# Another place for one weight tile, another order for sums and loads, in a three-stage fused kernel

## The chip, the cores and the metric

The kernel runs on one core of a Trainium2 chip. The metric is the device time of one execution in microseconds; the median of three runs before the change is 1219.49 us (1219.48 to 1224.46).

## What is computed

Three layers in float32, one after another, all in one program:

```python
# attention, q, k, v of 4 batches x 8 heads x 576 x 64, blocks of 64
attn = softmax(where(block_i >= block_j, q @ k.T / 8, -1e9));  y = attn @ v
x = y.transpose(0, 2, 1, 3).reshape(2304, 512)
# first block: 512 -> 768 -> 512
h = maximum(maximum(x @ w1, x @ w2), x @ w3);  x = h @ w_out
# second block: four experts, 512 -> 1024 -> 512
for e in range(4):  out += p[:, e:e+1] * (maximum(x @ w1[e], 0) @ w2[e])
```

## The kernel before

A float32 product is made of three matmuls: each operand is split into a rounded high part and the low rest, and high by high, high by low and low by high are added up in PSUM. Weights are kept split that way.

**Attention and the first block.** Attention goes by pairs of heads: 4 batches of 4 pairs (n = 0 to 15, NALL = 16). For a pair come scores (L159), minima on VectorE (L224), exponentials on ScalarE (L231), scaling by the row sums on GpSimd (L257), transposes on TensorE (L285) and the product with v (L320). While the pairs of batch b + 1 run, the first block of batch b (`moe1`, L547) fills TensorE's gaps: a generator cut into units of about four matmuls, and `filler.upto` (L698) says after each step of a pair how many units shall have been traced. `LAG` (L16) and a term that grows with n hold it back. The scheduler places instructions by priority (order of tracing) and by its own simulated times; each engine and each queue then works strictly in the placed order. `tc.issue_after(x)` queues what its block traces behind x, for instructions on the engine of x alone.

A batch in `moe1` has 18 tiles of its hidden layer: for weights w1, w2, w3 (n = 0, 1, 2) and rows ff = 0 to 5, each 12 matmuls (`mm3`, L488) of 128x512 into one of two PSUM banks. The eviction is a copy on ScalarE for n = 0 (L562) and a running maximum on VectorE for n = 1, 2 (L564). Then `moe1_out` (L537) makes the output in four parts d = 0 to 3, 18 matmuls each. Weight tiles come by DMA from the split copies `held` (L474), all on the SP queue: `wt` and `wu` (five buffers together) for the hidden layer, `wo` (two buffers) for the output layer.

**The fourth batch's first block** (`moe1_last`, L584) uses seven products of half-size blocks in place of eight (Strassen's scheme in Winograd's form), for 384 of its columns at a time; the columns that do not fit take a second, narrower run (`rh`, `wu`) of 18 matmuls per d. It needs sums and differences of weight blocks. These are made earlier by `sums(g, w0, w1)` (L516), for g = 0 to 8 (g = 3 * (ff // 2) + n), from the two weight tiles of rows ff - 1 and ff: two adds of 128x512 on VectorE (L522), four of 128x256 (L524 to L527), a rounding copy on ScalarE (L530), a subtraction on VectorE (L531), and a 1 MB store to `summed` (L532). They are worked out in places of the arena that are free then, the future results of batches 1 and 2. Batch 1 makes g = 0, 2, 4, 6, 8, batch 2 makes g = 1, 3, 5, 7. The adds are traced when the second tile of the pair has been evicted, but nothing binds them to that; the rounding copy is queued behind the next tile's eviction. In `moe1_last` the sums of a group come back into the places of `xh`, `xl` (8 KB per partition each) and two more in turn (L611 to L622); the ninth group uses `xh`. The output layer of the fourth batch takes its four tiles from the two `wo` buffers in turn, so d = 2 follows d = 0 and d = 3 follows d = 1.

**The second block** begins with e = 0. `hidden2` (L1013) makes seven products of six matmuls for a pair of row blocks n, `second` (L1074) the other layer. `weights_in(e, n)` (L970) loads e_w1[e, n] (512 KB) into one scratch tile `t`, makes three combinations on VectorE (L949 to L952), rounds on ScalarE (L956), subtracts on VectorE (L958) into one of two tiles `w`, and stores the result to `ka` (L982) for later passes. `weights_out(e, n)` (L985) does the like for e_w2[e, n] (load L988 into a part of `part`, results in `w2` and `part`), with GpSimd for the subtraction. `part` (L1343) is one tile of 3072 columns; it begins where `xh` began, and `xl` follows `xh`. Its pool `pe` has `reuse_waits="tile"`: a tile of it waits for the earlier tiles that it overlaps. Before, `weights_in(0, 1)` is traced at L1321, its load behind the last load of the first block.

Of the kernel before, what the change touches and what calls it, by code (L numbers as in the profile page):

```python
# [7 lines left out]
F32R = mybir.dt.float32r  # L8
# [4 lines left out]
ALU = mybir.AluOpType  # L13
AX = mybir.AxisListType

LAG = 9  # L16
# [5 lines left out]
P = 128  # L22
# [5 lines left out]
def program(tc, q, k, v, w123, w_out, probs, e_w1, e_w2, out):  # L28
    nc = tc.nc

    B, H, D, S = k.shape[0], 2 * k.shape[1], k.shape[2] // 2, k.shape[3]
# [3 lines left out]
    KD = DM // P  # L35
    NF = FF // P
    NPAIR = H // 2
# [5 lines left out]
    def f(ap):  # L43
        return ap.bitcast(F32)
# [16 lines left out]
    arena = big.tile([P, KD * NT], F32, name="arena")  # L61
    x2f = [arena[:, b * KD * S:(b + 1) * KD * S].rearrange("p (d s) -> p d s", d=KD) for b in range(B)]
    dram = root.enter_context(tc.tile_pool(name="dram", bufs=1, space=bass.MemoryType.DRAM))
    held = [dram.tile([P, 2, NF * P], F32, name=f"held{i}") for i in range(3 * NF + KD)]
    summed = [dram.tile([P, 2, 4, 2 * P], F32, name=f"summed{i}") for i in range(3 * NF // 2)]
# [11 lines left out]
    mp = moe.enter_context(tc.tile_pool(name="moe", bufs=1))  # L77
    MAIN = 512
# [7 lines left out]
    NGRP = 3 * NF // 2  # L86
# [10 lines left out]
    pairs, later, made, exps, normal, least = {}, [], {}, [], [], []  # L97
# [259 lines left out]
    for n, src in enumerate(tiles):  # L357
        A = src.shape[1]
# [102 lines left out]
    def moe_weight(b, n, at=0, a0=0):  # L461

        if b == 0:
            return convert.weight(n)
        A = tiles[n].shape[1]
        wide = n >= 3 * NF
        if b == B - 1 and not wide:
            if at == 0:
                taken[0] = 0
            if at % WT >= 3:  # L470
                wide = True
                taken[0] += 1
        wt = weight_tile(n, wide)
        made["load"] = nc.sync.dma_start(  # L474
            out=f(wt[:, :, a0:A].rearrange("p k a f -> p k (a f)")), in_=held[n][:, :, a0 * P:A * P]
        )
        return wt
# [15 lines left out]
    UNITS = 3 * NF * 3 + KD * 5  # L493
# [21 lines left out]

    def sums(g, w0, w1):  # L516

        o = (2 - (g // 2 % 2) * (g % 2 == 0)) * KD * S
        high, raw = (arena[:, o + i * 8 * P:o + (i + 1) * 8 * P] for i in range(2))
        for i, w in enumerate((w0, w1)):  # L520
            x = [w[:, j].rearrange("p a f -> p (a f)") for j in range(2)]
            nc.vector.tensor_tensor(raw[:, i * 4 * P:(i + 1) * 4 * P], f(x[0]), f(x[1]), op=ALU.add)  # L522
        a11, a12, a21, a22 = (raw[:, i * 2 * P:(i + 1) * 2 * P] for i in range(4))
        nc.vector.tensor_tensor(a22, a21, a22, op=ALU.add)  # L524
        nc.vector.tensor_tensor(a21, a11, a21, op=ALU.subtract)
        nc.vector.tensor_tensor(a11, a22, a11, op=ALU.subtract)
        nc.vector.tensor_tensor(a12, a12, a11, op=ALU.subtract)  # L527
        behind = yield
        with tc.issue_after(behind.ins):
            nc.scalar.copy(high.bitcast(F32R), raw)  # L530
        nc.vector.tensor_tensor(raw.bitcast(F32R), raw, high, op=ALU.subtract)  # L531
        nc.sync.dma_start(  # L532
            out=summed[g].rearrange("p x s f -> p (x s f)"), in_=arena[:, o:o + 16 * P]
        )
        yield

    def moe1_out(b, runs):  # L537
# [9 lines left out]
    def moe1(b):  # L547
        hidden = [mp.tile([P, NF, MAIN], F32R, name=x, tag=x) for x in ("hh", "hl")]
        hh, hl = ([x[:, ff] for ff in range(NF)] for x in hidden)
        xh, xl = xs[b]  # L550
        prev, last, under = {}, {}, []
        if b:
            order = [(2 * j + i, n) for j in range(NF // 2) for n in range(3) for i in range(2)]
        else:
            order = [(ff, n) for ff in range(NF) for n in range(3)]
        for at, (ff, n) in enumerate(order):
            wt = moe_weight(b, 3 * ff + n, at)
            m = ps_m.tile([P, 512], F32, name="m", tag="m")[:, 0:MAIN]
            yield from mm3(m, [(wt[:, 0, d], wt[:, 1, d], xh[:, d], xl[:, d]) for d in range(KD)])
            if n == 0:  # L560
                prev[ff] = mp.tile([P, MAIN], F32, name="mt", tag="mt", bufs=3)
                ins = nc.scalar.copy(prev[ff], m)  # L562
            else:
                ins = nc.vector.tensor_tensor(prev[ff], m, prev[ff], op=ALU.max)  # L564
            if under:
                under.pop().send(ins)
            t = prev[ff]
            if n == 2:
                nc.gpsimd.tensor_scalar(hh[ff], t, 1.0, 0.0, op0=ALU.mult, op1=ALU.add)
                nc.gpsimd.tensor_tensor(hl[ff], t, f(hh[ff]), op=ALU.subtract)  # L570
            if b and ff % 2:
                g = 3 * (ff // 2) + n
                if g % 2 == b - 1:
                    under.append(sums(g, last[0], wt))
                    next(under[0])
            last[0] = wt
            yield
        yield from moe1_out(b, [(MAIN, hh, hl, lambda d: x2f[b][:, d, 0:MAIN])])
        for x in under:
            x.send(made["out"])  # L580

    begun = [0]

# [126 lines left out]
    NALL = B * NPAIR  # L710
    filler = Filler()
# [24 lines left out]
    for n in range(NALL):  # L736
        b, d = divmod(n, NPAIR)
        ahead = n + 2 < NALL
        prep = prep_pair(n + 2) if ahead else iter(())
        g = 2 * n  # L740
        ta, tb = [[(turn_probs, g + h, part) for h in range(2)] for part in range(2)]
        va = (values, n)
        apart = n + 1 < 2 * NPAIR
        s0, s1, s2 = [(scores, n + 1, i) if n + 1 < NALL else (None,) for i in (0, 1 if apart else 3, 2)]
        pp = (next, prep, None)
        if apart:
            todo = [ta[0], s0, pp, tb[0], s1, ta[1], tb[1], s2, pp, va]
        else:
            todo = [ta[0], s0, pp, tb[0], ta[1], tb[1], s1, pp, va]
        for m, st in enumerate(todo):  # L750
            if d == NPAIR - 1 and m == 6:
                moe1_inputs(b, range(KD - 1))
            stage(*st)
            if b == 0 and m == 3 and n:
                weigh(n - 1, made["pv"])
            if d == NPAIR - 1 and m == len(todo) - 1:
                if b == 0:
                    weigh(n, made["pv"])
                moe1_inputs(b, [KD - 1])
            at = (n + (m + 1) / len(todo)) / NPAIR  # L760
            filler.upto((at - 1) * UNITS - LAG - 0.6 * max(0, n - NPAIR))
        if n + 4 < NALL:
            load_pair(n + 4)
        if d == NPAIR - 1:
            if b == 0:
                first.close()
                ps_m = ps.enter_context(tc.tile_pool(name="ps_m", bufs=2, space=PSUM, reuse_waits="tile"))
            if b < B - 1:
                filler.work.append(moe1(b))
# [64 lines left out]
    early = {}  # L834
# [135 lines left out]
    def weights_in(e, n, behind=None):  # L970

        w = xp.tile([P, 7, 2, QW_], F32R, name="w1", tag="w1", bufs=2)
        if (e, n) in stored:
            load(f(w[:]), kept1[e][n][:])
            return w
        stored.add((e, n))
        raw = scratch()[:, 0:7 * QW_].rearrange("x (n f) -> x n f", n=7)
        with tc.issue_after(behind.ins) if behind else nullcontext():
            nc.sync.dma_start(out=raw[:, 0:4], in_=e_w1[e, n])
        combos(*(raw[:, i] for i in (0, 1, 2, 3, 4, 5, 6, 3)))  # L980
        halves(w, raw, [(nc.vector, 0, 4), (nc.vector, 4, 7)])
        nc.sync.dma_start(out=kept1[e][n][:], in_=f(w[:]))  # L982
        return w

    def weights_out(e, n):  # L985
        w = tile_in(p2, "w2", W2_, F32R, 3)
        s, raw = parts["ws"], parts["raw"]
        nc.sync.dma_start(out=raw, in_=e_w2[e, n])  # L988
        mix_ = parts["mix"]
        cuts = [(nc.gpsimd, 0, 2), (nc.gpsimd, 2, 4)]  # L990
        combos(*(raw[:, i] for i in range(4)), *(mix_[:, i] for i in (1, 2, 3, 0)))
        halves(w, raw, cuts)
        halves(s, mix_, cuts)
        nc.sync.dma_start(out=kept2[e][:, 0:3, n], in_=f(w[:, 0:3]))
        stores.append(nc.sync.dma_start(out=kept2[e][:, 3:7, n], in_=f(s[:])))
        return w
# [317 lines left out]
    ready = [weights_in(0, 0, made["sums"])]  # L1314
# [3 lines left out]
    for _ in following:  # L1318
        filler.upto(filler.done + 3)
    filler.rest()  # L1320
    ready.append(weights_in(0, 1, made["load"]))  # L1321
    moe.close()
    ps.close()
    pools = ExitStack()
# [11 lines left out]
    def reserve(pool, tag, shape, dt, bufs=1):  # L1336
# [10 lines left out]
        raw=first_[:, 8 * QW_:12 * QW_].rearrange("x (n f) -> x n f", n=4),  # L1347
        mix=second_.rearrange("x (n f) -> x n f", n=4),
        hq00=first_.rearrange("x (n j s) -> x n j s", n=4, j=2),
        pb0=second_[:, 0:2 * CT].rearrange("x (c s) -> x c s", c=2),  # L1350
    )

    def temp():
        return pe.tile([P, CT], F32, name="tmp", tag="tmp", bufs=NTMP)
# [11 lines left out]
    for e in range(E):  # L1366
        for g in range(NG):
# [3 lines left out]
            for it in range(2):  # L1371
                n = 2 * g + it
# [3 lines left out]
                last = ends and it == 1  # L1376
                following = combine(*blocks(1)) if last else iter(())
                made = next(following) if last else None
# [128 lines left out]
```

## Time and profile before

| | us |
|---|---|
| median of the runs | 1219.49 |
| the profiled execution | 1223.43 |
| its span, first to last instruction | 1221.6 |
| TensorE busy in it | 1185.6 |
| VectorE busy in it | 901.7 |
| ScalarE busy in it | 486.5 |
| GpSimd busy in it | 280.2 |

The profile is that of one execution. The times of its rows are from the start of the span. The hidden layers of batches 0 to 2 lie, beside attention, up to about 399 us; the fourth batch's first block goes from there to 496 us; the second block follows. PE is TensorE's matmuls, PEld its weight loads, DVE is VectorE, ACT is ScalarE, POOL is GpSimd, SPq is the queue on which SyncE issues DMAs.

### The profile page before, as it was taken

What the parts mean: (1) busy time and instruction counts of PE and PEld (TensorE: products, weight loads), DVE (VectorE), ACT (ScalarE), POOL (GpSimd) and SP (SyncE); (2) the same over time, 40 slices, a digit from 0 to 9 for tenths busy, and PEclk for the clock granted to TensorE, in tenths of its full rate; (3) what the DMA queues carried; (4) which work ended last, traced back from release to release, by engine and by line L of the source; (5) the groups of instructions that cost most, each with busy time, mean ns of one, the idle gap of its engine ahead of it and who ended that gap; (6) DMA issues with size and microseconds to landing.
All of it is one profiled execution on the core that took longest, in us unless ns stands there. A gap on an engine that the chain in (4) does not pass through costs nothing.

```text
span 1221.6 us, 18277 instructions
## 1 busy us (share of the span) xinstructions
PE 1185.6 (97%) x6887; PEld 1066.6 (87%) x6887; DVE 901.7 (74%) x1570; ACT 486.5 (40%) x1008; POOL 280.2 (23%) x300
## 2 busy tenths in 40 slices
PE   7889999999999998999999999999999999999998
PEld 4567777777787997899999999999999999999998
DVE  4877876755654476798898895768787887586896
ACT  5976765445544123444344440233222223322222
POOL 2458852542341000333333340000000000000000
PEclk8999999999999999999999999999999999999999
DMA  5836765754644664688988865777887887676654
GB/s 205 276 133 218 250 217 194 237 164 157 222 167 187 215 205 166 253 332 322 354 327 317 307 240 193 285 288 276 350 299 306 322 305 268 241 271 230 252 211 176
DMA packets 84651, 303.51 MB, mean 248 GB/s; under 512 B 8972, under 2 KB 20564, under 8 KB 69460
## 3 DMA queue, kind: packets, MB, share of 16 engines
q1 hardware_dynamic: 84564, 302.35, 68.6%
q8 instruction: 54, 0.88, 0.3%
q14 instruction: 33, 0.27, 0.1%
HBM read 209.75 MB, written 92.57 MB: 247 GB/s over the span
## 4 chain that ended last, share of the span: by engine, by line
PE 85%; ACT 4%; DVE 4%; DMA 4%; POOL 2%; issue 1%; SPq 0%; DVEq 0%; POOLq 0%; ACTq 0%
PE m L1004 27%; PE o L1163 17%; PE m L488 14%; PE m L633 5%; PE o L1090 4%; PE o L1086 4%; PE o L1089 4%; PE tt L285 3%; PE pv L320 2%; PE st L187 2%; ACT p L231 2%; PE m L1163 2%; DMA w<-kb 1%; POOL p L257 1%; PE st L208 1%
## 5 line engine op out<-in xcount | busy, mean ns | idle before, releaser
L1004 PE MATMUL m<-t,w 128*128 128x384 f32 x1152 | 228.8, 336 | 0.0
L1163 PE MATMUL o<-hx,w 128*128 128x384 f32 x1176 | 226.0, 337 | 0.5 <-DMA w<-kb 0.5
L1163 PEld LDWEIGHTS o<-hx,w 128*128 128x128 f32 x1176 | 207.8, 188 | 0.8 <-PE m L1004 0.8
L1004 PEld LDWEIGHTS m<-t,w 128*128 128x128 f32 x1152 | 203.6, 188 | 2.9 <-DVE tmp L1024 0.2
L1004 PE MATMUL m<-b,w 128*128 128x384 f32 x864 | 175.8, 336 | 0.3 <-DVE w L958 0.3
L1004 PEld LDWEIGHTS m<-b,w 128*128 128x128 f32 x864 | 153.1, 188 | 3.8 <-DVE w L958 0.7
L231 ACT ACTIVATE p<-st,mn 128x128 f32<-128x128 f32 (+2 forms) x144 | 78.7, 558 | 62.7 <-DVE mn L224 62.6
L257 POOL TENSOR_SCALAR p<-p,sm 128x128 f32<-128x128 f32 (+4 forms) x108 | 75.0, 709 | 90.0 <-ACT high L125 32.5
L1024 DVE TENSOR_TENSOR tmp<-m,tmp 128x384 f32<-128x384 f32 x144 | 77.7, 550 | 21.4 <-PE m L1004 21.2
L958 POOL TENSOR_TENSOR w<-part,w 128x512 fp32r<-128x512 f32 x32 | 49.0, 1552 | 191.4 <-DVE mix L952 122.3
L488 PE MATMUL m<-xh,wt 128*128 128x512 f32 x256 | 87.0, 404 | 0.9 <-ACT mt L562 0.8
L1134 ACT CAST hx<-hq 128x768 fp32r<-128x768 f32 x49 | 40.6, 837 | 98.8 <-PE o L1163 75.8
L224 DVE TENSOR_REDUCE mn<-st 128x1 f32<-128x128 f32 (+2 forms) x144 | 67.8, 511 | 14.5 <-ACT p L231 7.3
L285 PE MATMUL tt<-ident,p 128*128 128x128 f32 x400 | 62.7, 290 | 16.0 <-ACT eh L295 6.5
L1086 PE MATMUL o<-w,hh 128*128 128x512 f32 x192 | 74.6, 391 | 0.5 <-ACT w L956 0.5
L1090 PE MATMUL o<-w,hl 128*128 128x512 f32 x192 | 74.9, 391 | 0.0
L1089 PE MATMUL o<-w,hh 128*128 128x512 f32 x192 | 74.8, 390 | 0.0
L285 PEld LDWEIGHTS tt<-ident,p 128*128 128x128 f32 x400 | 47.9, 147 | 29.9 <-ACT eh L295 8.2
L488 PE MATMUL m<-hh,wo 128*128 128x512 f32 x192 | 64.9, 405 | 4.9 <-DMA wo<-held 4.0
L958 POOL TENSOR_TENSOR part<-mix,part 128x512 fp32r<-128x512 f32 x32 | 44.7, 1405 | 67.1 <-ACT part L956 67.1
L1134 ACT CAST hx<-part 128x768 fp32r<-128x768 f32 x28 | 23.3, 836 | 91.5 <-PE o L1163 69.5
L1135 DVE TENSOR_TENSOR hx<-hq,hx 128x768 fp32r<-128x768 f32 x49 | 46.7, 955 | 16.0 <-ACT hx L1134 15.7
(225 smaller groups left out, 2258.1 us busy)
## 6 DMA issues: line engine op xcount, KB each, us to landing
w<-kb SPq DMA_DIRECT2D x55, 1024.0 KB, 5.7
w<-ka SPq DMA_DIRECT2D x28, 1792.0 KB, 7.5
ka<-w SPq DMA_DIRECT2D x16, 1792.0 KB, 6.7
kb<-part SPq DMA_DIRECT2D x16, 1024.0 KB, 6.6
wt<-held SPq DMA_DIRECT2D x28, 512.0 KB, 4.9
kb<-w SPq DMA_DIRECT2D x16, 768.0 KB, 5.3
arena<-in_w SPq DMA_DIRECT2D x18, 512.0 KB, 4.3
wo<-held SPq DMA_DIRECT2D x12, 768.0 KB, 4.9
```

The costliest lines, as they stand in the source:

```text
L224: least.append(nc.vector.tensor_reduce(mn[:, m:m + 1], x, axis=AX.X, op=ALU.min))
L231: exps.append(nc.scalar.activation(to, x, ACTF.Exp, bias=mn[:, m:m + 1], scale=-1.0, accum_out=sm[:, m:m + 1],))
L257: normal.append(nc.gpsimd.tensor_scalar(x, x, sm[:, c:c + 1], 1.0, op0=ALU.mult, op1=ALU.mult))
L285: nc.tensor.transpose(tt[:, c:c + P], pt[i][:, k0:k0 + P], ident)
L488: nc.tensor.matmul(out=out_, lhsT=w, rhs=x, start=m == 0, stop=m == n - 1)
L958: eng.tensor_tensor(w[:, a:b, 1], raw[:, a:b], f(w[:, a:b, 0]), op=ALU.subtract)
L1004: ins = nc.tensor.matmul(out=m, lhsT=a, rhs=b, start=start and n == 0, stop=stop and n == 3 * KH - 1, skip_group_check=True,)
L1024: nc.vector.tensor_tensor(t, x, y, op=ALU.add)
L1086: ins = nc.tensor.matmul(out=o, lhsT=hh[:, ts], rhs=wh, start=i == 0, stop=False)
L1089: nc.tensor.matmul(out=o, lhsT=hh[:, ts], rhs=wl, start=False, stop=False)
L1090: nc.tensor.matmul(out=o, lhsT=hl[:, ts], rhs=wh, start=False, stop=i == G - 1)
L1163: nc.tensor.matmul(out=o, lhsT=a, rhs=b, start=start and m == 0, stop=stop and m == 2, skip_group_check=True,)
```

## The change

In words, in the order of the diff: the weight tile of d = 2 in the fourth batch's output layer is loaded into the place of `xh`; the sums of odd groups and of g = 8 are made in batch 1 and the other even groups in batch 2, with another choice of the arena place; the first two adds are queued behind the eviction of the pair's second tile, and the store behind the weight load that was traced last when the tile after next is evicted; in the last pair, from its fifth step on, the filler may be five units further; the first load of the second layer's weights, e_w2[0, 0], is issued behind the load of d = 2, and `weights_in(0, 1)` is traced after it, its load queued behind it.

```diff
@@ moe_weight
         wide = n >= 3 * NF
+        if b == B - 1 and n == 3 * NF + 2:
+            wt = mp.tile([P, KD, MAIN], F32R, name="xh", tag="xh").rearrange("p d s -> p (d s)")
+            wt = wt[:, 0:2 * A * P].rearrange("p (k a f) -> p k a f", k=2, a=A)
+            made["early"] = nc.sync.dma_start(
+                out=f(wt.rearrange("p k a f -> p k (a f)")), in_=held[n][:, :, 0:A * P]
+            )
+            return wt
@@ sums
-        o = (2 - (g // 2 % 2) * (g % 2 == 0)) * KD * S
+        o = (2 - (g % 4 == 3)) * KD * S
         high, raw = (arena[:, o + i * 8 * P:o + (i + 1) * 8 * P] for i in range(2))
+        behind = yield
         for i, w in enumerate((w0, w1)):
             x = [w[:, j].rearrange("p a f -> p (a f)") for j in range(2)]
-            nc.vector.tensor_tensor(raw[:, i * 4 * P:(i + 1) * 4 * P], f(x[0]), f(x[1]), op=ALU.add)
+            with tc.issue_after(behind.ins):
+                nc.vector.tensor_tensor(raw[:, i * 4 * P:(i + 1) * 4 * P], f(x[0]), f(x[1]), op=ALU.add)
...
         nc.vector.tensor_tensor(raw.bitcast(F32R), raw, high, op=ALU.subtract)
-        nc.sync.dma_start(
-            out=summed[g].rearrange("p x s f -> p (x s f)"), in_=arena[:, o:o + 16 * P]
-        )
+        behind = yield
+        with tc.issue_after(behind.ins):
+            nc.sync.dma_start(
+                out=summed[g].rearrange("p x s f -> p (x s f)"), in_=arena[:, o:o + 16 * P]
+            )
         yield
@@ moe1
-            if under:
-                under.pop().send(ins)
+            for x in under[:]:
+                x[1] += 1
+                x[0].send(ins if x[1] == 2 else made["load"])
+                if x[1] == 3:
+                    under.remove(x)
...
-                if g % 2 == b - 1:
-                    under.append(sums(g, last[0], wt))
-                    next(under[0])
+                if (g % 2 or g == NGRP - 1) == (b == 1):
+                    under.append([sums(g, last[0], wt), 1])
+                    next(under[-1][0])
+                    under[-1][0].send(ins)
...
-        for x in under:
-            x.send(made["out"])
+        for x, at in under:
+            if at == 1:
+                x.send(made["out"])
+            x.send(made["load"])
@@ the loop over the pairs
-            filler.upto((at - 1) * UNITS - LAG - 0.6 * max(0, n - NPAIR))
+            lag = LAG + 0.6 * max(0, n - NPAIR) - 5 * (n == NALL - 1 and m > 3)
+            filler.upto((at - 1) * UNITS - lag)
@@ weights_out
-        nc.sync.dma_start(out=raw, in_=e_w2[e, n])
+        if e or n:
+            nc.sync.dma_start(out=raw, in_=e_w2[e, n])
@@ between the blocks
     filler.rest()
-    ready.append(weights_in(0, 1, made["load"]))
     moe.close()
...
+    with tc.issue_after(made["early"].ins):
+        made["load"] = nc.sync.dma_start(out=parts["raw"], in_=e_w2[0, 0])
+    ready.append(weights_in(0, 1, made["load"]))
```

## Rows read from the trace of the kernel before

**Rows 1.** The page, busy us (share of the span) and instructions.
```profile
PE 1185.6 (97%) x6887; PEld 1066.6 (87%) x6887; DVE 901.7 (74%) x1570; ACT 486.5 (40%) x1008; POOL 280.2 (23%) x300
```

**Rows 2.** Timeline of PE: start, us, engine, line, op, tiles, [idle before <-releaser].
```profile
188.88 1.09 PE L285 MATMUL tt<-ident,p 128*128 128x128 f32 x8 [0.76 <-POOL p L257]
...
215.55 1.19 PE L285 MATMUL tt<-ident,p 128*128 128x128 f32 x8 [1.92 <-POOL p L257]
...
304.89 0.50 PE L488 MATMUL m<-xh,wt 128*128 128x512 f32 x1 [0.79 <-ACT mt L562]
...
378.12 1.56 PE L285 MATMUL tt<-ident,p 128*128 128x128 f32 x10 [0.70 <-POOL p L257]
380.42 1.86 PE L285 MATMUL tt<-ident,p 128*128 128x128 f32 x15 [0.74 <-POOL p L257]
383.01 0.87 PE L320 MATMUL pv<-eh,vraw 128*64 128x384 f32 x4 [0.73 <-ACT eh L295]
...
481.83 0.50 PE L488 MATMUL m<-hh,wo 128*128 128x512 f32 x1 [3.85 <-DMA wo<-held]
...
503.11 0.51 PE L1086 MATMUL o<-w,hh 128*128 128x512 f32 x1 [0.53 <-ACT w L956]
...
510.01 2.02 PE L1004 MATMUL m<-b,w 128*128 128x384 f32 x10 [0.27 <-DVE w L958]
```

**Rows 3.** Windows: us, busy us of five engines, PEclk, DMA share, GB/s.
```profile
216.00:220.00 4.00, 4.00 (x15) 3.27 (x14) 3.42 (x5) 2.11 (x4) 3.69 (x5) 0.57 0.30 102
...
482.00:484.00 2.00, 2.00 (x7) 1.58 (x8) 0.00 (x0) 0.00 (x0) 0.00 (x0) 0.67 0.98 398
484.00:486.00 2.00, 2.00 (x6) 1.51 (x5) 0.76 (x2) 0.00 (x0) 0.00 (x0) 0.50 0.14 57
```

**Rows 4.** Timeline of the SP queue, 477 to 493 us: issues of DMAs.
```profile
477.56 0.79 SPq L474 DMA_DIRECT2D wo<-held  x2
478.40 0.42 SPq L979 DMA_DIRECT2D t<-in_e_w  x1
...
491.94 0.38 SPq L979 DMA_DIRECT2D t<-in_e_w  x1
492.38 0.90 SPq L988 DMA_DIRECT2D part<-in_e_w  x1
```

**Rows 5.** Timeline of PE: last products from xh, d = 3, second block.
```profile
466.97 1.21 PE L633 MATMUL m<-t,xh 128*128 128x384 f32 x6
...
489.80 0.40 PE L488 MATMUL m<-hh,wo 128*128 128x512 f32 x1
...
496.06 1.21 PE L1004 MATMUL m<-b,w 128*128 128x384 f32 x6
497.10 2.24 PE L1004 MATMUL m<-t,w 128*128 128x384 f32 x12
```

**Rows 6.** The page, DMA issues: KB each, median us to landing.
```profile
wo<-held SPq DMA_DIRECT2D x12, 768.0 KB, 4.9
```

**Rows 7.** Timeline of DVE, 485 to 500 us: weights of the second block.
```profile
485.20 0.42 DVE L949 TENSOR_TENSOR t<-t 128x256 f32<-128x256 f32 x1 [8.69 <-DMA t<-in_e_w]
...
489.41 2.09 DVE L958 TENSOR_TENSOR w<-t,w 128x1024 fp32r<-128x1024 f32 x2 [2.65 <-ACT w L956]
...
499.86 0.41 DVE L949 TENSOR_TENSOR t<-t 128x256 f32<-128x256 f32 x1
```

**Rows 8.** Groups by line (sums): busy us, mean ns, idle before <-releasers.
```profile
L522 DVE TENSOR_TENSOR arena<-wt 128x512 f32<-128x512 f32 x11 | 7.9, 722 | 11.2 <-DMA wt<-held 7.1 <-DMA summed<-arena 3.9 <-ACT arena L406 0.2
L522 DVE TENSOR_TENSOR arena<-wu 128x512 f32<-128x512 f32 x7 | 5.1, 744 | 12.3 <-DMA wu<-held 8.7 <-DMA summed<-arena 3.6
...
L527 DVE TENSOR_TENSOR arena<-arena 128x256 f32<-128x256 f32 x9 | 4.2, 468 | 0.1
```

**Rows 9.** Timeline of DVE and ACT, 205 to 212 us.
```profile
209.89 0.69 DVE L522 TENSOR_TENSOR arena<-wu 128x512 f32<-128x512 f32 x1 [4.02 <-DMA wu<-held]
...
211.00 0.47 ACT L231 ACTIVATE p<-st,mn 128x256 f32<-128x256 f32 x1 [3.77 <-DVE mn L224]
```

## The prediction

> **What bounds the kernel now.** Read first the busy shares: TensorE is busy for 97% of the span [rows 1], so a change can gain only where TensorE stands still, or runs at a low clock, and only in the stages that the edits touch. Next read TensorE's timeline for idle time ahead of an instruction, over 160 to 520 us: that is where batches two to four of the first layer block and the start of the second block lie. Nine waits matter [rows 2]; the bracket gives their length and what ended them. Three stand inside the sums' stage (0.76 at 188.88, 1.92 at 215.55, 0.79 at 304.89), three in the tail of the last attention pair (0.70, 0.74, 0.73), one in the fourth batch's output layer (3.85 at 481.83, ended by the load of a wo tile), two at the second block's start (0.53, 0.27). Then the windows: after the waits of 1.92 and 3.85 us the granted clock fell to 0.57 over 216 to 220, to 0.67 over 482 to 484 and to 0.50 (that is 1.2 GHz) over 484 to 486 [rows 3]. After 510 TensorE is all but gapless, so what is gained earlier reaches the end, if the second block's weights keep up.
>
> All sums go against the profiled execution: 1223.43 us, that is its span of 1221.6 and 1.83 around it. It stands 3.94 above the median of the runs, 1219.49.
>
> **The third place for wo (d = 2).** Before, d = 2 loads into the place of d = 0. The SP queue issues both last wo loads at 477.56 [rows 4], when d = 0 and d = 1 end together, and TensorE waits 3.85 us. After, d = 2 goes into xh, last read by the ninth group's products, whose last six begin at 466.97 [rows 5] and are over some 1.1 us later. A wo load lands 4.9 us after its issue [rows 6], so at about 473, before 477.6. The wait goes. What is late next is d = 3: it still waits for d = 0, is issued at 477.56 and lands at 482.5. It is wanted after d = 2, and one d takes 496.06 - 489.80 = 6.26 us [rows 5], so at 483.8: 1.3 us of margin. The low clock behind the wait goes too: 2 x (1 - 0.67) + 2 x (1 - 0.50) = 1.66 us. Gain 3.85 + 1.66 = 5.5 us, bounds 0 (d = 3 just as late) and 5.5.
>
> **The order of second-block loads.** With that, TensorE reaches the second block at 490.5 instead of 496.06, and the 0.80 us of waits there say that its weights come just in time. Before, SP issued the load of e_w1[0,1] (t) at 478.40, behind the two wo loads, t for [0,2] at 491.94 and e_w2[0,0] (part) at 492.38 [rows 4]. After, part comes first and t is queued behind it. But part is one tile of 3072 columns; it begins where xh begins and covers xh and half of xl, and its pool waits by whole tiles. So the load of part should wait until d = 2 is done with xh, at 483.8, and t behind it on the same queue, though t's own buffer is free: issue near 484.3, 5.9 us later than now.
>
> Does that hurt? The chain of [0,1]: 485.20 - 478.40 = 6.8 us to landing, then 485.20 to 491.50 (489.41 + 2.09), 6.3 us of combining and rounding, of which 2.65 is a wait that ScalarE ended [rows 7]. From 484.3 the weights are ready at 497.4 at the latest, at 494.7 without the wait. They are wanted after the first seven products: 42 matmuls of 0.173 us each (497.10 - 496.06 for six, [rows 5]), near 498. So no stall there. The next chain, [0,2], begins with its store and its load at about 495 to 497.8 instead of 491.94; its load was taken up 499.86 - 491.94 = 7.9 us later [rows 4, 7]. Ready 6.8 + 3.65 to 7.9 + 6.3 later: 505.5 to 512, the first half 1.04 sooner. TensorE ran out of other work 510.01 - 496.06 - 0.53 - 0.27 = 13.15 us after its start [rows 2, 5], so at 503.7; part comes eight microseconds earlier than now, which lets some 1.6 us of second-layer products move up (7 of 12 not yet used, 0.23 each), so 505.3. The new wait lies between 0 and 6 us and takes the place of 0.80. I take 1.2, near the rows of now, since I read most of the 2.65 as ScalarE standing behind the eviction of d = 2, which the 3.85 us wait had delayed: +0.4 us, bounds -0.8 and +6.9 (with 1.7 of low clock).
>
> **Sums behind evictions, odd groups first.** A sum's two adds (0.72, 0.74 us) stood on VectorE as soon as they could be ordered, ahead of their tiles' products; VectorE idled 7.1 + 8.7 us there for weights and 3.9 + 3.6 for a stored sum's place [rows 8]. What that does: at 209.89 it had stood 4.02 us for a weight tile, the minima behind it came late, and ScalarE's exponentials idled 3.77 [rows 9]; GpSimd's products followed, and TensorE lost 1.92 at 215.55 and 4 x (1 - 0.57) = 1.72 of clock [rows 2, 3]: 3.64 us. After, the adds are queued behind the eviction of their second tile, when both tiles have long landed. But the order binds on one engine only: a group with n = 0 (three of nine) is evicted by ScalarE, and its adds on VectorE stay free. So I count two thirds of 3.64, 2.4, and half of each of 0.76 and 0.79: 3.2 us, bounds 5.2 and -2 (each sum's 2 x 0.73 + 4 x 0.47 = 3.3 us on VectorE now comes in one block behind an eviction and can hold up a minimum there). What is queued behind the new waits: on VectorE the next reductions, covered by 12 products per tile; on SP the store of a sum behind a weight load that was issued long ago, at nothing. The odd groups first only move the third stop, at 304.89, where a sum waited for the store before it.
>
> **Filler five units earlier in the last pair.** 18 products (5 units) of d = 1 that ran after the attention may now run inside it, where 0.70 + 0.74 + 0.73 = 2.17 us stand idle. The first wait precedes the place where they are traced; I count 1.47 and half of 0.70: 1.8 us, bounds 2.2 and -1.2 (a product of 0.4 us ahead of each of three runs). 36 products stay to hide the fourth batch's inputs.
>
> **Sum.** -5.5 + 0.4 - 3.2 - 1.8 = -10.1 us: 1213.3 from the profiled time, 1209.4 from the median. Part of the 3.94 between them may be the stop at 215 itself, which would then not be there to gain in most runs; two of three runs stand at the median, so I stay near the lower figure: 1210.5 us, own range 1206 to 1214.
>
> **Rivals.** (a) The second block's weights take the place of the wait: part waits for d = 2, t behind it, [0,2] is late by 4 us and the clock falls for 1.7, less the 0.80 of now: +4.9 in place of +0.4, 1215 us. For it: all three loads share one queue, and 0.80 us of waits now. Against it: one wo load fewer beside them, and the 6.3 us holds a wait that goes. "DMA: Bandwidth & Descriptors" of the Trainium skill (section Anatomy of one DMA) says that a semaphore wait stands on the issuing sequencer before dispatch; that is the mechanism of this rival, and the trace agrees where t is issued at 478.40 right behind wo. (b) The sums' stops move and do not vanish: gain 0 there, 1213.7 us. For it: VectorE's work is the same, only 1.92 of the stops was ended by a late weight tile. (c) Slower: a pair's tiles stay in use until VectorE's adds behind the second eviction, not only until the products. Five buffers, a tile every 12 x 0.232 = 2.8 us (0.232 from 6.26 us for 18 products and 18 of half width): of five tiles two are held, three tiles are 8.3 us, less 1.5 for the adds and 4.9 for a load [rows 6]: 2 us of slack. Once a load takes over 6.9 us TensorE waits at each of the six bound groups, 3.64 us each by the stop at 215: 21.8 lost, 7 gained elsewhere, 1234 us. Against it: attention's work between the tiles lengthens the slack. (d) d = 3 comes later than its 1.3 us of margin, since loads beside it share the engines: 3 us given back, 1213.5.
>
> **Chances.** Forecast 0.55, (a) 0.14, (b) 0.16, (c) 0.09, (d) 0.06. A measurement can tell about 0.5%, 6.1 us, from no change, so faster means under 1213.4: nearly all of the forecast's share, and less than half of (a), (b) and (d): 0.63. Slower (over 1225.6) is (c): 0.09. The rest 0.28. Range 1205 to 1219: it takes in (a), (b) and (d), leaves out (c) and a sum with every bound at its best.
>
> **What would show it.** No wo wait near 480 and a granted clock of 1.00 there; the early wo load issued near 468; VectorE idle ahead of the sums' adds down from 23.5 us to under 8; no wait of over 1 us at 205 to 220; TensorE gapless from 377 to 386. Part issued before the products of d = 2 begin would prove my reading of the tile's wait wrong, and make the second block safer. Wrong altogether: TensorE waiting more than 3 us for w in the second block, or for wt or wu in batches two and three.

## The result and the profile after

The median of the changed kernel is 1230.83 us (1227.22 to 1235.01, 7 runs) against 1223.2 us before, in runs beside it: ratio 1.0067, 95% interval 1.0045 to 1.0089. It is slower by 0.7%, clear of noise, and outside the range of the forecast. The profiled execution took 1230.84 us, its span is 1229.0: 7.4 us more than that of before.

Where the 7.4 us are is seen by cutting the span at three marks: the wo stop that `ACT wo L100` ends (173.54 after, 172.90 before), which lies ahead of nearly all that the edits touch; the first matmul of the second block (L1023 after, L1004 before); the first matmul of its second pass (L1182 after, L1163 before). TensorE's timeline of after at the first, second and third mark (start, us, engine, line, op, tiles, [idle before <- releaser]):

```profile
173.54 0.50 PE L495 MATMUL m<-hh,wo 128*128 128x512 f32 x1 [0.88 <-ACT wo L100]
...
490.20 1.03 PE L1023 MATMUL m<-b,w 128*128 128x384 f32 x5
...
774.29 0.59 PE L1182 MATMUL o<-hx,w 128*128 128x384 f32 x2
```

and of before (the second one stands in [rows 5]):

```profile
172.90 0.50 PE L488 MATMUL m<-hh,wo 128*128 128x512 f32 x1 [0.88 <-ACT wo L100]
...
767.37 0.41 PE L1163 MATMUL o<-hx,w 128*128 128x384 f32 x1 [0.50 <-DMA w<-kb]
```

| stretch, us | before | after | difference |
|---|---|---|---|
| start to first mark | 172.9 | 173.5 | +0.6 |
| **first block**: first to second mark | 323.2 | 316.7 | -6.5 |
| **first pass** of the second block | 271.3 | 284.1 | +12.8 |
| from there to the end | 454.2 | 454.7 | +0.5 |

So 6.5 of the 10.5 us forecast for the first block came, and the first pass of the second block lost twice as much. TensorE stands idle 9.7 us in it (before 1.3), and its matmuls are busy for 274.4 us (before 270.0). No edit takes work into that pass. Its largest stops, in TensorE's timeline of after (before had the two of 0.53 and 0.27 in [rows 2], and 0.50 at its end):

```profile
498.20 0.49 PE L1109 MATMUL o<-w,hl 128*128 128x512 f32 x1 [1.02 <-DVE hl L1084]
499.82 1.31 PE L1023 MATMUL m<-t,w 128*128 128x384 f32 x6 [1.12 <-DVE tmp L1043]
507.03 1.33 PE L1023 MATMUL m<-t,w 128*128 128x384 f32 x6 [1.06 <-DVE tmp L1043]
...
707.56 0.62 PE L1023 MATMUL m<-b,w 128*128 128x384 f32 x2 [1.23 <-ACT tmp L1048]
...
734.00 1.34 PE L1023 MATMUL m<-t,w 128*128 128x384 f32 x5 [3.43 <-DVE tmp L1043]
```

VectorE ended 7.3 of the pass's 9.6 us of stops, and the two latest stand 200 us behind the last edit. At the latest one VectorE was not idle: the eviction that TensorE waits for (L1043) stood behind other work (VectorE, after), and the granted clock was 0.60 over 734 to 738:

```profile
730.33 2.02 DVE L880 TENSOR_TENSOR t<-arena,t 128x768 f32<-128x768 f32 x1
...
733.40 0.54 DVE L1043 TENSOR_TENSOR tmp<-m,tmp 128x384 f32<-128x384 f32 x1
```

The queue of SP and VectorE's timeline say what happened at the start (after; compare [rows 4, 7]):

```profile
479.48 0.32 SPq L481 DMA_DIRECT2D wo<-held  x1
482.76 0.33 SPq L1372 DMA_DIRECT2D part<-in_e_w  x1
483.18 0.38 SPq L997 DMA_DIRECT2D t<-in_e_w  x1
...
502.64 0.42 SPq L997 DMA_DIRECT2D t<-in_e_w  x1
```

```profile
486.49 0.42 DVE L970 TENSOR_TENSOR mix<-part 128x256 f32<-128x256 f32 x1
492.55 0.56 DVE L1043 TENSOR_TENSOR tmp<-m,tmp 128x384 f32<-128x384 f32 x1 [5.64 <-PE m L1023]
493.03 1.12 DVE L968 TENSOR_TENSOR mix<-mix,part 128x256 f32<-128x256 f32 x1
494.07 0.55 DVE L1043 TENSOR_TENSOR tmp<-m,tmp 128x384 f32<-128x384 f32 x1
494.54 1.04 DVE L967 TENSOR_TENSOR t<-t 128x256 f32<-128x256 f32 x1
495.51 1.50 DVE L969 TENSOR_TENSOR mix<-part,mix 128x256 f32<-128x256 f32 x1
...
500.15 2.08 DVE L976 TENSOR_TENSOR w<-t,w 128x1024 fp32r<-128x1024 f32 x2
```

Part waited for d = 2 and t stood behind it, 4.8 us later than before (483.18 for 478.40). But VectorE did not take t when it had landed (at 487.37): it stood 5.64 us for the second block's own first product (L1043 evicts it), since in the placed order that eviction comes ahead of the combinations of t. Before, the combinations for [0,1] came first [rows 7]. So w is ready at 502.2 in place of 491.5, and the next t is issued at 502.64 in place of 491.94.

### The profile page after: what moved, and what is told of

It is laid out like the page before. It is cut to its first block, busy times and chain, and to the rows that moved or that the text cites. A ratio compares the mean times of both kernels' runs of the same rounds, so it can differ in the third digit from the quotient of the medians.

```text
span 1229.0 us, 18284 instructions
## 1 busy us (share of the span) xinstructions
PE 1187.8 (97%) x6887; PEld 1067.8 (87%) x6887; DVE 910.4 (74%) x1570; ACT 486.4 (40%) x1008; POOL 286.5 (23%) x300
## 4 chain that ended last, share of the span: by engine, by line
PE 77%; DVE 10%; DMA 5%; ACT 4%; issue 2%; POOL 1%; SPq 0%; DVEq 0%; ACTq 0%; POOLq 0%
PE m L1023 24%; PE o L1182 17%; PE m L495 15%; PE m L650 5%; PE tt L285 3%; PE st L187 3%; PE pv L320 2%; PE m L1182 2%; PE o L1105 2%; PE o L1108 2%; PE o L1109 2%; DMA t<-in_e_w 2%; ACT p L231 2%; DVE w L976 1%; DMA part<-in_e_w 1%
## 5 line engine op out<-in xcount | busy, mean ns | idle before, releaser
L1023 PE MATMUL m<-t,w 128*128 128x384 f32 x1152 | 229.7, 338 | 5.6 <-DVE tmp L1043 5.6
L1182 PE MATMUL o<-hx,w 128*128 128x384 f32 x1176 | 226.1, 337 | 0.1
L1023 PEld LDWEIGHTS m<-t,w 128*128 128x128 f32 x1152 | 203.7, 188 | 9.4 <-DVE tmp L1043 7.5
L1182 PEld LDWEIGHTS o<-hx,w 128*128 128x128 f32 x1176 | 207.9, 188 | 0.4 <-PE m L1023 0.4
L1023 PE MATMUL m<-b,w 128*128 128x384 f32 x864 | 178.5, 338 | 1.2 <-ACT tmp L1048 1.2
L1023 PEld LDWEIGHTS m<-b,w 128*128 128x128 f32 x864 | 154.0, 189 | 4.8 <-ACT tmp L1048 1.6
L1043 DVE TENSOR_TENSOR tmp<-m,tmp 128x384 f32<-128x384 f32 x144 | 77.8, 551 | 28.0 <-PE m L1023 24.3
L495 PE MATMUL m<-hh,wo 128*128 128x512 f32 x180 | 58.9, 397 | 2.0 <-DMA wo<-held 1.1
```

What stands on the lines that cost most here:

```text
L495: nc.tensor.matmul(out=out_, lhsT=w, rhs=x, start=m == 0, stop=m == n - 1)
L1023: ins = nc.tensor.matmul(out=m, lhsT=a, rhs=b, start=start and n == 0, stop=stop and n == 3 * KH - 1, skip_group_check=True,)
L1043: nc.vector.tensor_tensor(t, x, y, op=ALU.add)
L1182: nc.tensor.matmul(out=o, lhsT=a, rhs=b, start=start and m == 0, stop=stop and m == 2, skip_group_check=True,)
```

## The experiments

Two causes were thus open: the loads come late, or the scheduler has placed the pass in another, worse order. The table has every kernel that was run: start of the second block and length of its first pass in the profiled execution, median, and ratio to before with its interval.

| kernel | start | first pass | median | ratio |
|---|---|---|---|---|
| before | 496.1 | 271.3 | 1223.2 to 1224.3 | 1 |
| after | 490.2 | 284.1 | 1230.83 | 1.0067 (1.0045 to 1.0089) |
| e1, after without the load order | 490.5 | 285.0 | 1233.61 | 1.0074 (1.0057 to 1.0090) |
| e2, load order alone | 496.1 | 282.4 | 1236.90 | 1.0103 (1.0086 to 1.0120) |
| e3, third place alone | 486.1 | 291.1 | 1237.60 | 1.0106 (1.0087 to 1.0125) |
| e4, sums alone | 495.2 | 272.8 | 1225.22 | 1.0006 (0.9993 to 1.0019) |
| e5, filler alone | 492.3 | 278.0 | 1227.02 | 1.0035 (1.0022 to 1.0048) |
| p3, before in the order of after | 498.2 | 286.0 | 1240.63 | 1.0135 (1.0122 to 1.0148) |
| p2, after in the order of before | 491.5 | 280.8 | 1228.03 | 1.0034 (1.0021 to 1.0047) |
| p4, e1 in the order of before | 490.1 | 282.7 | 1228.98 | 1.0042 (1.0028 to 1.0057) |
| p5, place and filler, order of before | 493.0 | 280.9 | 1227.11 | 1.0030 (1.0018 to 1.0042) |
| q1, after with t early | 492.0 | 274.6 | 1222.07 | 0.9987 (0.9975 to 0.9999) |
| q2, q1 in the order of before | 491.1 | 274.2 | 1221.51 | 0.9980 (0.9968 to 0.9992) |
| q4, q2 without the load order | 491.3 | 272.6 | 1220.98 | 0.9980 (0.9967 to 0.9993) |
| r1, q1 in the order of after | 490.4 | 285.1 | 1232.15 | 1.0076 (1.0057 to 1.0094) |
| r3, q4 without the sums' edits | 490.8 | 274.6 | 1218.48 | 0.9960 (0.9942 to 0.9978) |

In the profiled execution of e3 the first mark already stands 4.0 us earlier than in before, so its start is 6.0 and not 10 us better.

**One edit at a time.** e1 takes the load order out of after; e2 to e4 put one edit alone into before.

```diff
 e1 (from after)
-        if e or n:
-            nc.sync.dma_start(out=raw, in_=e_w2[e, n])
+        nc.sync.dma_start(out=raw, in_=e_w2[e, n])
+    ready.append(weights_in(0, 1, made["load"]))
     moe.close()
 ... (and the three new lines behind the pools go)
 e2 (from before): the edits of weights_out and between the blocks, with
+    with tc.issue_after(made["load"].ins):
+        made["load"] = nc.sync.dma_start(out=parts["raw"], in_=e_w2[0, 0])
```

> The changed kernel without its new order of second-block loads (the load of t again behind the last wo load, part after it); third place, sums and filler stay. Theory 1 (the new load order costs the time: it makes t late and puts VectorE's combinations of t behind the first evictions of the second block): the second block starts at 490 +-1.5 us as in the changed kernel, TensorE loses under 2.5 us over 490 to 560 in place of 7.9, and the time falls by 5.5 to 12 us to 1219 to 1225.5 (the far end if the stops at 707 and 734 go too). Theory 2 (the loss has nothing to do with the loads: the scheduler has placed everything behind batch 1 in another order because the sums moved): 7 us are still lost over 490 to 560, time 1229 to 1232.

> The kernel before with the new load order alone: part issued behind the last wo load, t behind part, wo in its old two places; xh is free long before, so part has no tile to wait for and t is issued some 0.5 us later than before, near 479. Theory 1a (the loss is VectorE's placed order: combinations of part and the first evictions ahead of the combinations of t): TensorE loses 5 to 8 us over the first 60 us of the second block, against 1.7 before; time 1227 to 1230. Theory 1b (the loss is the whole-tile wait of part for d = 2, with t behind it): no such wait here, so at most 0.5 us is lost, 1223 to 1224. In the changed kernel both held at once; this run parts them.

> The kernel before with the third place for the tile of d = 2 alone. By the prediction's term: the stop of 3.85 us ahead of d = 2 and its low clock go, second block at 490.6 (5.5 earlier), 1217.7. If d = 3 is late as in the changed kernel (1.12 us): 1219. If the second block's weights take its place because the start comes 5 us earlier while t is issued no earlier: the gain shrinks to 0 to 2 us, 1221 to 1223.

> The kernel before with the sums' edits alone (odd groups and g = 8 in batch 1, adds behind the eviction, stores behind a later load). By the prediction's term: 3.2 us gained over 180 to 320, 1220. By the rival that the stops only move, which the changed kernel's trace speaks for (1.92 at 215 gone, 2.43 at 300 come): 0 +-1 us, 1222.5 to 1224. If the stops at 707 and 734 of the changed kernel come from the scheduler's reshuffle by the sums: some 5 us lost over 680 to 760, 1227 to 1229.

Theory 1 of e1 fell: without the load order the pass is as long (285.0). The time of theory 2 came, to 1.6 us, but not its reason: the sums alone leave the pass at 272.8 (e4). e2 lost more than either of its theories said, and e3 is 15 us slower than the slowest that was expected. e2 shows that the load order alone lengthens it by 11.1 us, with t issued only 0.6 us later than before and no tile to wait for:

```profile
478.49 0.42 SPq L1354 DMA_DIRECT2D part<-in_e_w  x1
479.00 0.73 SPq L979 DMA_DIRECT2D t<-in_e_w  x1
```

And e3, which touches no load of the second block, lengthens it by 19.8. Setting the placed instructions side by side shows what moved. VectorE's order from the first eviction of the second block on is the same, instruction for instruction, in e2 and after; it is the same in e1 and e3; these two orders and that of before all differ (compared by line and tiles, 225 and 234 of the 910 instructions of before fall out of the common order). The orders of e4, e5 and q1 are others again (some 100 to 125 out), though e4's costs only 1.5 us. So each edit made the scheduler place the pass anew; that its simulated times are the reason is taken from how it works, and no run here shows it. e2, with after's order, has two of the stops shown above, 1.12 and 3.43, to 0.02 us, 5.7 to 5.9 us later:

```profile
505.71 2.26 PE L1005 MATMUL m<-t,w 128*128 128x384 f32 x6 [1.11 <-DVE tmp L1025]
...
739.70 1.31 PE L1005 MATMUL m<-t,w 128*128 128x384 f32 x6 [3.41 <-DVE tmp L1025]
```

e4 shows the sums' edits to be worth nothing, as the rival (b) had it.

**The order by itself.** The new theory: the placed order of the pass costs the time. To test it, an order was imposed. At the end of tracing, each instruction of the second block (from the combinations of t for [0,1] on) is queued behind the one that precedes it, on its engine, in another kernel's placed order; four engines are held so, SP is not. In the traces VectorE's order then is that of the other kernel, but for one place. The edit in short:

```diff
+    for engine, order in ORDERS.items():   # places in the order of tracing
+        made = [i for i in nc.cur_bb.bb.instructions if i.engine is engine]
+        made = [made[n] for n in order]
+        for a, b in zip(made, made[1:]):
+            tc.add_manual_dep(b, a.name, NoSync, reason="order")
```

> The changed kernel, all its edits in it, but VectorE, ScalarE, GpSimd and TensorE take the instructions of the second block (from the combinations of t for [0,1] on) in the order in which the kernel before has them; the queue of SP is left as the changed kernel has it. Theory 1 (the loss is the placed order that the scheduler made of the second block, not the time at which loads come): the 12.8 us lost over 500 to 775 fall to 3 to 6 (2.7 before, and up to 3 for t issued near 483 in place of 478), time 1219 to 1223. Theory 2 (the loads come late, by part's wait for d = 2 and t behind it): 12 us stay lost, 1229 to 1232.

> The mirror of it: the kernel before with none of the edits, t loaded first as before and no tile to wait for, but the four engines take the second block in the order of the changed kernel. Theory 1 (the placed order): 10 to 14 us lost over 500 to 775, with stops near 498 to 510 and near 710 and 735; time 1233 to 1238. Theory 2 (late loads): nothing is late, 1223 to 1226.

> The changed kernel without the new order of second-block loads (third place, sums and filler stay) with the second block in the order of the kernel before. Without that order it took 1233.6. Theory 1 (the placed order): the start at 490.5 is kept to the end, 1216 to 1220, faster than before. Theory 2 (a start 5.6 us earlier finds the weights and VectorE 5.6 us too late, whatever the order): 5 to 6 us are lost at the first two products' weights, 1222 to 1225.

> The kernel before with the third place for the tile of d = 2 and the filler's five units, no edit to the sums or to the loads, and the second block in the order of the kernel before. Theory 1 (the placed order): the gains ahead of 496 us are kept, 1214 to 1218. Theory 2 (the early start meets late weights): 1220 to 1224. Against the kernel with the sums' edits beside it (p4) it also tells what the sums give: by the prediction's term p4 is 3 us faster, by the rival that their stops only move the two are within 1.5 us.

p3 settles that the order is enough: none of the edits is in it, the first t is issued 17.8 us ahead of the second block (480.40; before 17.7), and the pass takes 286.0 us, the kernel 1240.63. The queue of SP was not held and follows the engines: part is issued at 480.88 in place of 492.38, and the next t, which waits for w, at 510.65 in place of 491.94. No run imposes a kernel's own order on it, so the price of imposing is not known by itself; but e2 has the same order on VectorE with nothing imposed and loses 11.1 us, and the kernels with an order imposed and t early (q2, q4, r3 below) have passes of 272.6 to 274.6. Its stops are those of after once more (here the latest):

```profile
742.13 1.15 PE L1007 MATMUL m<-t,w 128*128 128x384 f32 x5 [3.42 <-DVE tmp L1027]
```

p2, p4 and p5 missed the forecast of the order theory by 5 to 9 us, and that of the other theory by 1 to 4 us: with the order of before the late stops go, but within 16 us of its start the second block loses more than its early start had won, in one or two stops. In p2 (TensorE, then VectorE, then SP):

```profile
506.61 1.65 PE L1026 MATMUL m<-t,w 128*128 128x384 f32 x4 [8.35 <-DVE tmp L1046]
```

```profile
495.06 1.01 DVE L1046 TENSOR_TENSOR tmp<-m,tmp 128x384 f32<-128x384 f32 x2
503.40 0.42 DVE L970 TENSOR_TENSOR t<-t 128x256 f32<-128x256 f32 x1 [7.33 <-DMA t<-in_e_w]
```

```profile
484.47 0.38 SPq L1000 DMA_DIRECT2D t<-in_e_w  x1
495.17 0.33 SPq L1003 DMA_DIRECT2D ka<-w  x1
495.55 0.42 SPq L1000 DMA_DIRECT2D t<-in_e_w  x1
```

The order of before has the combinations of t for [0,2] right behind the first two evictions. That t is issued when w for [0,1] is done (495.55) and lands at 503.4; VectorE stands for it, and the evictions behind it stand too. So there is a second cause, the late loads. p4, whose t for [0,1] is issued at 479.70, has it as well.

**The loads by themselves.** q1 changes one queue order in after; q2 and r1 hold it to the two orders; q4 is q2 with part loaded where before loads it; e5 is the filler's term in before.

```diff
-    with tc.issue_after(made["early"].ins):
-        made["load"] = nc.sync.dma_start(out=parts["raw"], in_=e_w2[0, 0])
-    ready.append(weights_in(0, 1, made["load"]))
+    ready.append(weights_in(0, 1, made["early"]))
+    with tc.issue_after(made["load"].ins):
+        made["load"] = nc.sync.dma_start(out=parts["raw"], in_=e_w2[0, 0])
```

> The changed kernel with one queue order altered: the load of t for [0,1] is queued right behind the early wo load (issue near 467.5, t free since 455) and part behind the last wo load, ahead of nothing of t. The placed order of the four engines is the scheduler's own; on VectorE the combinations of t now stand ahead of the first evictions of the second block. Theory 1 (placed order, and under it late weights: both go here): w for [0,1] ready near 485, t for [0,2] issued near 483 in place of 502.6, lost over 500 to 560 under 1.5 us in place of 5.2; what is left is what the new order does further on, 0 to 5 us; time 1217 to 1224. Theory 2 (an early start of the second block always ends at VectorE's or the queue's limit within its first products): 6 to 9 us lost over 495 to 515, 1226 to 1230.

> The same with the four engines' order of the second block as in the kernel before. With that order and t issued at 480 to 483 the third product stood 8.5 us for the combinations of t for [0,2], whose load landed at 500 beside the store of w and part. Theory 1 (t for [0,2] is late because its turn starts with t for [0,1]): w for [0,1] near 485, t for [0,2] issued near 483 and landed by 494, so the 8.5 us go and the start at 490 to 491.5 is kept to the end: 1216 to 1220. Theory 2 (the transfers of w, part and t together need till 500 whenever they start): 5 to 8 us lost there, 1224 to 1228.

> The same again, but part is loaded where the kernel before loads it, behind the store of w for [0,1]. If the early part matters by itself, the first products of the second layer stand 2 to 4 us for w2 as in the run without the new load order (3.9 us at 500), 1220 to 1223; if only t's lateness did, it is within 1 us of the run with part early, 1216 to 1220.

> The kernel before with the filler's five units alone. By the prediction's term 1.8 us gained, over 377 to 386, if the rest stays: 1221.5 to 1222.5. By the placed order, which this edit changes too from the second block on (about half as far from before's as the load order does): the gain there, and 0 to 8 us lost over 500 to 775; 1222 to 1230.

> The changed kernel with the load of t for [0,1] early (behind the early wo load), but the four engines held to the changed kernel's own order of the second block. The fourth corner of a square: order of the changed kernel with t late 1230.8, order of before with t late 1228.0, order of before with t early 1221.5. Theory 1 (the order costs by itself, whenever t comes): the early t gives back 0 to 3 us at the start and the stops at 498 to 516, near 545 and near 710 and 735 stay, 1228 to 1231. Theory 2 (only t's lateness costs; the order does no harm once t is early): 1221 to 1223.

> The kernel before with the third place, the filler's five units and t early, in the order of before, without the sums' edits; with them it took 1220.98. If the sums' edits are worth nothing (their own run gave a ratio of 1.0006): 1220 to 1222. If they are worth the 3.2 us of the prediction once the rest keeps what they gain: 1224.

With t issued at 475 to 477 the pass takes 272.6 to 274.6 us in the order of before, and 274.6 in the order that the scheduler then makes of itself (q1). The expected 467.5 was too early: in q1 the queue waited 7.3 us for VectorE's last use of the scratch tile t. The next t then lands before VectorE turns to it, without a wait (q4; SP, then VectorE):

```profile
476.03 0.33 SPq L1000 DMA_DIRECT2D t<-in_e_w  x1
484.86 0.38 SPq L1000 DMA_DIRECT2D t<-in_e_w  x1
```

```profile
479.91 0.43 DVE L970 TENSOR_TENSOR t<-t 128x256 f32<-128x256 f32 x1 [3.43 <-DMA t<-in_e_w]
495.13 0.41 DVE L970 TENSOR_TENSOR t<-t 128x256 f32<-128x256 f32 x1
```

What an early part is worth, q2 and q4 do not tell: part is issued behind the second t in both, at 484.49 and 485.34. The medians of q2, q4 and r1 lie 1.0 to 1.5 us above the ranges given for the theory that fits them, those of q1 and e5 inside theirs. r1 is the fourth corner: order of after, t early, 1232.15. The square of medians is

| | t late | t early |
|---|---|---|
| order of after | 1230.83 | 1232.15 |
| order of before | 1228.03 | 1221.51 |

The corner of after is the kernel itself, with nothing imposed. In the order of after an early t gives nothing, since VectorE takes it no sooner; r1 issues the next t at 502.79:

```profile
475.02 0.33 SPq L1000 DMA_DIRECT2D t<-in_e_w  x1
...
502.79 0.42 SPq L1000 DMA_DIRECT2D t<-in_e_w  x1
```

With t late, changing the order gives back 2.8 us. Both together give 9.3. (By the ratios to the runs of before beside each, 4 and 11 us.) e5 has the pattern where no load is touched: the filler shortens the way to the second block (below), its pass grows by 6.7 us in yet another order, and the kernel is slower; how much of the 6.7 is order and how much lateness was not parted there.

r3, third place, filler and early t in the order of before, has the lowest median: 1218.48 us, ratio 0.9960 (0.9942 to 0.9978), below both of its forecasts; its interval overlaps those of q2 and q4. The two largest stops from 480 us on that are left in it are for the wo tile of d = 3 and for one eviction that stands behind two slow combinations on VectorE:

```profile
484.42 0.47 PE L498 MATMUL m<-hh,wo 128*128 128x512 f32 x1 [1.11 <-DMA wo<-held]
499.86 1.80 PE L1015 MATMUL m<-t,w 128*128 128x384 f32 x6 [2.35 <-DVE tmp L1035]
```

## Why the prediction was wrong

- **The step that failed** is "After 510 TensorE is all but gapless, so what is gained earlier reaches the end, if the second block's weights keep up", and with it the +0.4 us for "The order of second-block loads" (bounds -0.8 and +6.9). The term measured 12.8 us, in the first pass. The step took the instructions of that pass as they stood in the trace of before and moved only the times of three loads. The order itself came out of the scheduler, and each of the edits here made another one; after's costs 11.1 us of the pass in e2 and 14.7 in p3. The prediction had no term and no rival for it, although the account of the kernel ahead of it says that the scheduler places by simulated times.
- **The base.** The forecast time was worked from 1219.49, the median of three runs. The five groups of 7 to 30 runs of before that stand beside the kernels here have medians of 1223.2 to 1224.3, so about 4 us of the miss in the time lie here and in no edit.
- **A reading that hid it.** "Its load was taken up 499.86 - 491.94 = 7.9 us later" was counted as the time of the load. The row has no idle time ahead of it: VectorE came from evictions, so it says when VectorE turned to t. The number was nearly right by luck (the load landed at 499.46), but the same reading failed for [0,1]: "The weights are ready at 497.4 at the latest" assumed that VectorE takes t when it lands; t landed at 487.37, its first combination ran at 494.54, and the weights were ready at 502.2.
- **Rival (a)** had its mechanism right: part waited for d = 2 (its last products end at 482.73), t behind it, issue at 482.76 and 483.18 where 484.3 was worked out. The queue's wait ahead of part was 2.9 us, ended by TensorE, and t had none of its own: VectorE's last use of it ended at 474.7. Its price, +4.9, is about half of what p2 shows where only the lateness acts: a stop of 8.35 us, a pass longer by 9.5.
- **What one execution can tell.** From the first mark to the stop at 304.89, the profiled executions of before, e2, e3, e5, p3, p5 and r3 run the same 818 matmuls in the same order, and no edit of theirs reaches there. They took 130.8 to 132.6 us for it, before 132.0. The stop of 1.92 at 215.55 is 0.89 to 2.46 long in them, and the clock behind it, 0.57 in before, stays at 1.00 in five of the seven. So the 3.64 us that the term of the sums starts from was in part that execution's own, and about 1 us of the gains in the first block that follow is no gain of an edit.
- **Third place**, -5.5: right in kind. e3's first block (first to second mark) takes 486.13 - 168.92 = 317.2 us, 6.0 less than before, 5.0 of them behind 304.89. In after the stop of 3.85 is gone and one of 1.12 is there instead, for d = 3. Rival (d) said that it would come late, but for another reason: the load took 4.2 us, no longer than usual (4.9 in [rows 6]), and was issued at 479.48, not 477.56, since products of d = 2 now stand among those of d = 0. The clock stayed up (timeline, then windows):

```profile
483.85 0.47 PE L495 MATMUL m<-hh,wo 128*128 128x512 f32 x1 [1.12 <-DMA wo<-held]
```

```profile
482.00:484.00 2.00, 0.88 (x8) 0.70 (x7) 0.00 (x0) 0.37 (x1) 0.00 (x0) 1.00 0.58 235
484.00:486.00 2.00, 2.00 (x9) 1.62 (x10) 0.00 (x0) 0.00 (x0) 0.00 (x0) 1.00 0.97 342
```

- **Sums**, -3.2: wrong. e4's first block is 0.6 us shorter (495.23 - 172.62 = 322.6), the kernel's ratio 1.0006; without them r3's median is the best. The adds hardly wait any more (18 adds, 3.7 us of idle time in place of 23.5 [rows 8], 3.0 of it for weight tiles in place of 15.8), but the stops moved, as rival (b) said: 1.92 at 215.55 became 0.46, and a new one came with a low clock behind it, 2.42 to 2.44 us long in every kernel with these edits (timeline, then window):

```profile
218.78 1.09 PE L285 MATMUL tt<-ident,p 128*128 128x128 f32 x8 [0.46 <-POOL p L257]
...
299.77 1.09 PE L285 MATMUL tt<-ident,p 128*128 128x128 f32 x8 [2.43 <-POOL p L257]
```

```profile
300.00:304.00 4.00, 4.00 (x24) 3.11 (x23) 3.88 (x10) 1.05 (x2) 3.49 (x4) 0.66 0.47 197
```

- **Filler**, -1.8: right in kind and about in size. e5's first block takes 492.25 - 172.59 = 319.7, 3.5 less, 2.3 of them behind 304.89; of the three stops of 2.17 us one of 0.73 is left, in e5 and in after. What the term left out: in all but e1 of the kernels with this edit TensorE stands 0.17 to 2.98 us for a weight tile at 427 to 431, in before and the kernels without it not at all. The terms do not add up: 6.0, 3.5 and 0.6 alone, 6.5 together.
- **Rival (c)** did not come: in batches two and three no such stop at each of the six groups stands in the trace of after; its longest is the 2.43 above.

## What to carry to other kernels

Where a scheduler places work by simulated times, the order of every later stage belongs to the change: compare the placed instructions of each engine before pricing an edit, and do not carry a gain across a stage whose order has moved. Another order need not be a worse one (e4, q1), so it has to be measured. To learn what an edit itself is worth, hold the later stage to the old order, and the other way round put the new order into the old kernel: the square of the two parts them. A gain in start time reaches the end only if the loads that the next stage wants first also start that much sooner.

## What the runs showed of the hardware

An add on VectorE with two operands in SBUF took 0.42 us alone and 1.04 to 1.50 us while GpSimd was subtracting (the rows of VectorE at 493.03 to 495.51 above; GpSimd's rows of after are these), and the eviction at 494.07, which reads one operand from PSUM, kept its 0.55:

```profile
492.58 2.72 POOL L976 TENSOR_TENSOR w<-part,w 128x512 fp32r<-128x512 f32 x2 [111.29 <-PE m L1023]
495.27 1.46 POOL L976 TENSOR_TENSOR part<-mix,part 128x512 fp32r<-128x512 f32 x1
```

"SBUF — State Buffer" of the Trainium skill (section Who interferes with whom) says that a VectorE instruction with two SBUF inputs contends with a GpSimd instruction that reads SBUF; the trace agrees. It makes the order on VectorE dearer still, since a slow combination ahead of an eviction holds TensorE: in r3 two of 1.46 and 1.48 us stand ahead of the eviction that ends the stop of 2.35.

VectorE, idle for it each time, took up the load of t (512 KB) 3.6 to 3.9 us after its issue when it ran alone (q1, q2, q4, r3; in q4 476.03 to 479.91 above), 5.3 us after it when issued 0.4 us behind the load of one wo tile (p4, 479.70 to 484.98), 6.8 behind two of them (before, 478.40 to 485.20), and 10.2 beside the store of w and the load of part (p4, 490.29 to 500.53).
